# Feature-map attention and a soft mixture of experts: middle tiles summed in halves of 64 rows, with a bank of their own

## The chip, the cores and the metric

The kernel runs on one NeuronCore of a Trainium2 chip, in one launch. The metric is the device time of that launch in microseconds (us): the median of the runs. The profile is one further execution; its span goes from the first to the last instruction of the program. The engines are PE (TensorE; its weight loads are listed as PEld), DVE (VectorE), ACT (ScalarE), POOL (GpSimd) and SP (SyncE), which issues nearly all transfers.

## The reference

Linear attention over 8 batches, 8 heads, 576 tokens and 64 dimensions, then a soft mixture of 8 experts with 4 slots each over the 4608 resulting rows of 512. Everything is float32. The first part is where the change lies:

```python
def phi(x):
    proj = np.einsum('bhsd,df->bhsf', x, w_phi)          # w_phi: 64 x 128
    proj = proj - np.max(np.abs(proj), axis=-1, keepdims=True)
    return np.concatenate([np.exp(proj), np.exp(-proj)], axis=-1)
q_p, k_p = phi(q), phi(k)
kv = np.einsum('bhsf,bhsd->bhfd', k_p, v)                # per head: 256 x 64
z = np.sum(k_p, axis=2)
num = np.einsum('bhsf,bhfd->bhsd', q_p, kv)
den = np.einsum('bhsf,bhf->bhs', q_p, z)[..., None] + 1e-06
attn = num / den
# then, on x = attn as 4608 x 512:
logits = x @ phi                                         # 512 x 32
slot_input = softmax(logits, axis=0).T @ x
slot_out[e] = relu(slot_input[e] @ w1[e]) @ w2[e]        # 8 experts, 4 slots each
out = softmax(logits, axis=1) @ slot_out
```

## The kernel before, in words

Two batches of one head make a unit `u` (32 units). Its 2 x 576 = 1152 tokens are nine tiles of 128 tokens, so the fifth tile, number 4, holds the last 64 tokens of the first batch in rows 0 to 63 and the first 64 of the second batch in rows 64 to 127. It is called the middle tile. The projections work on blocks `b` of four tiles, 72 in all, without regard to units; `pieces` lists the stretches of a block that lie in one unit.

What happens to a block and a unit, with the lines of the profile:

- `proj` (L281): PE multiplies w_phi with the keys of block b on one half of the 64 + 64 rows, and the queries of block b - 2 on the other half. Results are psk (features by column) and psq (features by row).
- `kmax` (L286, DVE) and `kfac` (L289, L290, ACT): the largest absolute value per token, and its two exponentials. `kneg_exp`, `kpos_exp` (L312, L315, ACT): the features kf. `qabs` (L343, DVE), `qpos`, `qneg` (L348, L351, ACT): the same for queries.
- `vals` (L301, POOL): the values, with a column of ones at the end (65 columns), times both exponentials, one copy for each sign, into vs. The value tile vt comes from memory with ten blocks of 65 columns for the nine tiles: the middle tile is there twice, once with zeros in rows 64 to 127 and once with zeros in rows 0 to 63.
- `kvmm` (L328, PE): for each tile, sign and half of the 128 features one matmul of 64 stationary and 65 moving columns adds to kvp, which holds [sign, batch, 65] for the unit in one PSUM bank. For the middle tile the moving side is 130 columns wide, so that the two zeroed copies go into both batches at once.
- `kvcopy` (L337): one copy of kvp, 260 columns, to kvs, by DVE and ACT in the turn d, a, a, d.
- `num` (L381, PE): query features times kvs, in groups of three tiles. `scale`, `comb` (L392, L397, DVE), `denom` (POOL), `recip` (DVE, L412) and `divide` (POOL, L427) finish the rows of x.

After each half of the 8 heads' rows the logits of four tiles are formed (transposes to psx at L734, psl at L438) and the running softmax is kept. After the last unit follow the last logits (zturn to zsi; `zst` at L629 and L631 multiplies pieces of acc, 128 stationary columns, by 32 or 1 moving columns), then both expert layers (hp L850, yp L925) and the outputs (pso L945).

The order of the work is written out by hand: `ORDER` is a string of one letter per step (`LETTERS`), and the steps are issued in just this order on every engine. `Plan.add` gives each step its predecessors (`after`) and the buffers that it takes (`get`) and gives back (`put`); these only check the string. The costs in `add` are not used when the kernel is built. PSUM banks: two for psk, two for psq, one for kvp, and three (`nm`) which num, transposes, logits and slot sums share.

Of the kernel before, what the change touches and what calls it, by code (L numbers as in the profile page):

```python
# [56 lines left out]
class Plan:
# [42 lines left out]
ORDER = (  # L100
    "bcceafeefedhdggehjibecikbajelfcmdbmdknghjefomilcbunhfipoghclrjqddlrmkjagmjsnbkifnthijgvovmwcljofpwqdgcrvrmkjwnlm"
    "yhksomfdpnathixrvwvczolijwgfcrlhaqkdAvAgrmjnAbkwfbyomstizhcArfvwnlkjnAdorimdavAgcowhjpiqvcgwdfbmhgjyrlrdslxjztvf"
    "AknmivhiknawgowmcofjplcAhrjrAmdvqwxdlgjiykfrnakmgmostcvnbhpvjiwwlfocdjzqsArlvhkntrgbmdwAAvwomkfigcdryjharvznfkmi"
    "bowcvlpwjrghAqrmdnlijAAykofsmnhiczotxjvwgkdlvcfmgAwjqfjparrhsdmnmvgAtwAojlxihmkvyzwnorvjwpbrvwcfAixckmybdfazAnrh"
    "AdgliABABgjljCoqxcBCskhtBCmilmnfCdrDEkonvchpFwgvlwqoibcrrjdjkafbAnmhodsvkmwBitgCBcBvwCxlBylCfrnhfjrivmvhCwjDGdzx"
    "oEcwaqkipsndoFcgglHGjHIJrIymfKhKkAgldnqgbtLisojmArAvwfhkvimtpnjcojwzcrfalhvdgrmdwlkfAAnmAbjmJvwhoprkvMwyirjgjzcv"
    "wnlyAoifcdamdkqAnmlhixgzfoxsAtjrhjLviwrcgvlbmknoArfawvAjpqwxhycmklfbmnshrkdzidAtnorvcwAlivggjocmfajwrqMAprjdvhwk"
    "mknsdiynmgrAtzjfAogclvAwhoAljfiqdvgcwmrhkjpdvsftwxlnryvmgimazwrhkbjvowrnaiAvAmjpwocckymfnzdbAAhrdglBNjlCBgoiqCkf"
    "cBbsBAjmthAifmlnCrCdkhnvjiwxvwoDcoaEcBpbFbdgflBjxhrdCrNmvqxmskfnwCiBlCBhtgCojicaGxvfklDrnwdohxOrEkgnjFqvwiymvpcw"
    "gocHjHdzmIfgyrzJGkIsdlKLhnKmAfArjhlAmtvwiovAkiwAcnAjobacpqdgfglsrrvhmfjbknltwvOwmdyrvkjjgnraxvwimwzphocikocdfyrl"  # L110
    "ghirAdjqnlkszPxAAmfonojtmjvhwigmcvwdMjpcNArrflagkdmqhnsimfgljAkhAmvtwjopcfvyrJwjbirlanqdzkmAmAvvhnocsoAMiwtwbgcf"
    "yzbAjralNlfvhwAkrdiAmdkpnbxnvoghroqvjgwjcwdfsligycxtrdkzhvrminmvoAfjlmawgjcrfLApwlbjhvkqwryhmkAminzonAsBBcodticA"
    "gCCvdfjwBCfBrlrhlCAdkvniokhmjvnqxiwbDgwcoOEcFBBprlglsajytdmCmvjmxqknCfwPzHpgBIBjChmCrsjdgjfoPJvrkiDwhvEwKncFiMbd"
    "fGAohcHLylrtlgkaIqmAmJndsgKoijcfAzvwrdNkpvfwnrbvmAwahjhlirogAAtriknvjwvcwGyfOljzxkdonoxcmmghlqpriAvwbkrbjdysxAmA"
    "tznrcfhvgkndvwiwjofcaAlAlmmrhgpqdAkvfrjmwsnMohriitayLckvocvnwgrkdwnvjwxmjzffAglmplocyhjhAzNocxxAAqRldSRlmjrsmgkS"
    "APjOtPvmqprwvRrwSnvwiOTURsAQRkSotyrSnRvoVQwRVzrSSrvwyyTAARUzPASvzARXASwyXRYzA4XZYSY0X2QYZ0TZ73W905Q5682236573Q5+"
    "695W5888++8/W+<=/Q!=!i!!")

# [7 lines left out]
def tile_kernel(ctx: ExitStack, tc, xT, vv, w, phi, w1, w2, cst, out):  # L126
# [166 lines left out]
    def vals(p):  # L293
        b, u, t0, t1 = pieces[p]
        v = vt[u].rearrange("p (t e) -> p t e", e=65)
        if b not in vs:
            vs[b] = vp.tile([128, 2, 5, 65], F32, tag="vs", name="vs", bufs=BUFS["vs"])
        g = NT * u - 4 * b
        for t, n, o in (t0, min(t1, 5) - t0, 0), (max(t0, 4), t1 - max(t0, 4), 1):
            if n > 0:  # L300
                nc.gpsimd.tensor_tensor(vs[b][:, :, place(b, u, t, o):place(b, u, t, o) + n],  # L301
                                        v[:, t + o:t + o + n].unsqueeze(1).broadcast_to([128, 2, n, 65]),
                                        km[b][:, 0:2, g + t:g + t + n].unsqueeze(3).broadcast_to([128, 2, n, 65]), op=ALU.mult)

    def place(b, u, t, o):

        g = NT * u + t
        return g - 4 * b + (o if t == 4 else any(x % NT == 4 for x in range(4 * b, g)))

# [7 lines left out]
    def kvmm(p):  # L317
        b, u, t0, t1 = pieces[p]
        if t0 == 0:
            kvp[u] = pkv.tile([128, 2, 2, 65], F32, tag="kv", name="kvp")  # L320
        ps = kvp[u].rearrange("p a b e -> p a (b e)")
        v2 = vs[b].rearrange("p a t e -> p a (t e)")
        for t in range(t0, t1):
            o, m = 65 * (t > 4), 130 if t == 4 else 65
            at = 65 * place(b, u, t, 0)
            for pn in range(2):
                for f in range(0, FE, FE // 2):
                    nc.tensor.matmul(  # L328
                        ps[f:f + FE // 2, pn, o:o + m],
                        kf[b][:, pn, NT * u + t - 4 * b, f:f + FE // 2],  # L330
                        v2[:, pn, at:at + m],
                        start=(t == 0 and pn == 0), stop=(t == NT - 1 and pn == 1),
                        skip_group_check=True)

    def kvcopy(u, d):
        kvs[u] = qp.tile([128, 2, 2, 65], F32, tag="kvs", name="kvs")
        (nc.vector.tensor_copy if d else nc.scalar.copy)(kvs[u], kvp.pop(u))  # L337

# [675 lines left out]
```

## Time and profile before

| | |
|---|---|
| median of 3 runs | 329.23 us (328.81 to 330.84) |
| the profiled execution's own time | 328.39 us |
| its span | 326.6 us, mean granted TensorE clock 0.993 |
| busy: PE, PEld, DVE, ACT, POOL | 315.7, 269.4, 241.2, 229.3, 160.9 us |
| kvmm on PE (L328) | 2304 records, from 10.5 to 254.2 us |
| num on PE (L381) | 2304 records |
| projections on PE (L281) | 576 + 576 records |

A matmul of the program in float32 leaves two records in the profile, each with its weight load. A shape such as "128\*64 128x65" is rows by columns of the stationary operand, then rows by columns of the moving one. Two matmuls on different halves of the array (128\*64: different columns; 64\*128: different rows) can run side by side, so durations of records add up to more than the time; starts tell how fast they follow each other.

### The profile page before, as it was taken

To read this page: it belongs to the slowest core of one execution; us is meant where nothing else is said; L and a number is where in the kernel's file an instruction comes from. 1 tells how busy PE (TensorE), PEld (TensorE's weight loads), DVE (VectorE), ACT (ScalarE), POOL (GpSimd) and SP (SyncE) were. 2 spreads that over 40 slices of the span, in tenths; PEclk is the share of its full clock that TensorE was granted. 3 is DMA by queue.
4 is the path that set the end of the run, shared out by engine and by line. 5 is a ranking of instruction groups with operands and counts; after the bars stand their busy time and mean duration, and the time that the engine had idled before them with its cause. 6 is when DMAs were issued, how large, how long until landed. Compare 5 with 4: busy or idle time off the path is not lost.

```text
span 326.6 us, 16706 instructions
## 1 busy us (share of the span) xinstructions
PE 315.7 (97%) x7095; PEld 269.4 (82%) x7095; DVE 241.2 (74%) x688; ACT 229.3 (70%) x674; POOL 160.9 (49%) x339
## 2 busy tenths in 40 slices
PE   8999999999999999999999999999999999999990
...
GB/s 248 198 173 175 171 207 121 235 198 207 215 96 185 199 204 141 235 171 244 169 170 174 174 225 192 223 51 237 188 223 258 320 354 310 412 409 366 323 377 298
DMA packets 23130, 74.12 MB, mean 227 GB/s; under 512 B 2576, under 2 KB 2960, under 8 KB 23056
## 3 DMA queue, kind: packets, MB, share of 16 engines
...
q10 hardware_dynamic: 288, 0.40, 0.4%
q14 instruction: 18, 0.15, 0.1%
...
## 4 chain that ended last, share of the span: by engine, by line
PE 93%; DVE 1%; ACT 1%; issue 1%; DMA 1%; SPq 0%; DVEq 0%; POOL 0%; ACTq 0%; POOLq 0%
PE kvp L328 24%; PE psn L381 22%; PE psq L281 12%; PE psk L281 11%; PE psx L734 5%; PE yp L925 4%; PE hp L850 4%; PE psl L438 3%; PE pso L945 2%; PE pss L470 2%; PE psw L206 2%; DMA out<-o 1%; PE psd L463 1%; PE pss L585 1%; PE psh L903 1%
## 5 line engine op out<-in xcount | busy, mean ns | idle before, releaser
L301 POOL TENSOR_TENSOR vs<-vt,mk 128x520 f32<-128x520 f32 (+3 forms) x128 | 91.5, 730 | 59.5 <-ACT mk L290 42.5
L328 PE MATMUL kvp<-vs,kf 128*64 128x65 f32 (+1 forms) x2304 | 85.7, 229 | 0.0
L328 PEld LDWEIGHTS kvp<-vs,kf 128*64 128x64 f32 x2304 | 78.6, 138 | 4.7 <-issue 1.9
L381 PE MATMUL psn<-kvs,qf 128*64 128x65 f32 x2304 | 79.2, 223 | 0.3 <-issue 0.2
L381 PEld LDWEIGHTS psn<-kvs,qf 128*64 128x64 f32 x2304 | 72.6, 138 | 4.5 <-issue 1.0
L281 PE MATMUL psq<-xs,wd 64*128 64x128 f32 x576 | 75.5, 280 | 0.0
L281 PE MATMUL psk<-wd,xs 64*128 64x128 f32 x576 | 75.3, 280 | 0.1
L281 PEld LDWEIGHTS psq<-xs,wd 64*128 64x128 f32 x576 | 67.2, 187 | 4.1 <-issue 2.1
L281 PEld LDWEIGHTS psk<-wd,xs 64*128 64x128 f32 x576 | 67.0, 187 | 3.1 <-issue 1.6
L286 DVE TENSOR_REDUCE mk<-psk 128x4 f32<-128x512 f32 x72 | 48.2, 679 | 15.9 <-ACT kf L312 9.1
L312 ACT ACTIVATE kf<-psk 128x512 f32<-128x512 f32 x72 | 42.6, 594 | 22.5 <-PE psk L281 8.0
L343 DVE TRANSPOSE_TENSOR_REDUCE mts<-psq 128x16 f32<-128x512 f32 x72 | 50.2, 706 | 8.2 <-PE psq L281 3.5
L348 ACT ACTIVATE qf<-psq 128x512 f32<-128x512 f32 x72 | 42.4, 592 | 10.7 <-PE psn L381 3.0
L427 POOL TENSOR_TENSOR xc<-un,dn 128x256 f32<-128x256 f32 x62 | 37.9, 614 | 13.3 <-DVE dn L412 7.0
L351 ACT ACTIVATE qf<-psq 128x512 f32<-128x512 f32 x72 | 42.4, 594 | 1.7 <-DVE mts L343 1.7
L315 ACT ACTIVATE kf<-psk 128x512 f32<-128x512 f32 x72 | 42.6, 595 | 0.5 <-DVE mk L286 0.5
L392 DVE TENSOR_TENSOR un<-psn,eq 128x195 f32<-128x195 f32 x96 | 33.0, 350 | 10.3 <-PE psn L381 7.5
L397 DVE TENSOR_TENSOR un<-psn,un 128x195 f32<-128x195 f32 x96 | 33.4, 354 | 1.9
L359 ACT ACTIVATE mh<-mts 32x36 f32<-32x36 f32 x128 | 29.4, 229 | 2.4 <-DVE mts L343 0.6
L365 DVE TENSOR_REDUCE eq<-mh 32x9 f32<-32x36 f32 x128 | 26.1, 204 | 5.2 <-ACT mh L359 3.9
L949 DVE COPY o<-pso 128x384 f32<-128x384 f32 x24 | 12.1, 552 | 13.0 <-PE pso L945 13.0
L949 ACT COPY o<-pso 128x384 f32<-128x384 f32 x24 | 10.2, 484 | 11.7 <-PE pso L945 10.7
...
## 6 DMA issues: line engine op xcount, KB each, us to landing
...
```

The lines of the kernel that those rows point to most:

```text
L281: nc.tensor.matmul(ps, l, r, start=True, stop=True)
L286: nc.vector.tensor_reduce(km[b][:, 2], kx[b], axis=AX, op=ALU.max, apply_absolute_value=True)
L301: nc.gpsimd.tensor_tensor(vs[b][:, :, place(b, u, t, o):place(b, u, t, o) + n], v[:, t + o:t + o + n].unsqueeze(1).broadcast_to([128, 2, n ...
L312: nc.scalar.activation(kf[b][:, 1], kx[b], AF.Exp, scale=-1.0)
L315: nc.scalar.activation(kf[b][:, 0], kx[b], AF.Exp)
L328: nc.tensor.matmul(ps[f:f + FE // 2, pn, o:o + m], kf[b][:, pn, NT * u + t - 4 * b, f:f + FE // 2], v2[:, pn, at:at + m], start=(t == 0 an ...
L343: nc.vector.tensor_reduce(mts.rearrange("p r j -> p j r")[:, o:o + 4], qx[b].rearrange("p j (r t) -> p (j r) t", t=32), axis=AX, op=ALU.ma ...
L348: nc.scalar.activation(qf[b][:, 0], qx[b], AF.Exp)
L351: nc.scalar.activation(qf[b][:, 1], qx[b], AF.Exp, scale=-1.0)
L381: nc.tensor.matmul(ps[64 * f:64 * f + 64, j, pn], q2[:, pn, 64 * f:64 * f + 64], kv[:, pn, b2], start=True, stop=True)
L397: nc.vector.tensor_tensor(x, nx.pop(s)[:, :, 1], x, op=ALU.add)
L427: divider(u).tensor_tensor(x[:, :, h * D:(h + 1) * D], un[u][:, a:b, 0:64], dn[u][:, a:b].unsqueeze(2).broadcast_to([128, b - a, 64]), op= ...
```

## The change

- The values come with nine blocks of 65 columns, without the zeroed copies (`VW` 585 in place of 650), vs holds four tiles in place of five, and `vals` is one POOL instruction a piece.
- `kvmm` leaves out the middle tile. A new step `mid` does it in halves of 64 rows: for each sign, rows 0 to 63 add to the first batch in kvp with all 128 features as stationary columns, and rows 64 to 127 write the second batch's share into a bank of its own, psi (`half`), one of the three shared `nm` banks.
- `kvcopy` is cut in three: `mcopy` (ACT) copies psi to part2; `kvcopy` (always ACT now) copies the first batch's half of kvp; `kvadd` (DVE) adds part2 to the second batch's half. The first num group of a unit needs kvcopy, the others kvadd.
- `kf` and `vs` are given back by a step of no work, `kfree`, after kvmm and mid.
- `ORDER` is written anew throughout.

```diff
-VW = 10 * 65
+VW = NT * 65
+VSW = 2 * 4 * 65
@@ vals
-            vs[b] = vp.tile([128, 2, 5, 65], F32, tag="vs", name="vs", bufs=BUFS["vs"])
-        for t, n, o in (t0, min(t1, 5) - t0, 0), (max(t0, 4), t1 - max(t0, 4), 1):
-            if n > 0:
-                nc.gpsimd.tensor_tensor(vs[b][:, :, place(b, u, t, o):place(b, u, t, o) + n],
...
+            vs[b] = vp.tile([128, 2, 4, 65], F32, tag="vs", name="vs", bufs=BUFS["vs"])
+        g, n = NT * u - 4 * b, t1 - t0
+        nc.gpsimd.tensor_tensor(vs[b][:, :, g + t0:g + t1],
...
@@ kvmm
-            o, m = 65 * (t > 4), 130 if t == 4 else 65
-            for pn in range(2):
+            for pn in range(2) if t != 4 else ():
                 for f in range(0, FE, FE // 2):
                     nc.tensor.matmul(
-                        ps[f:f + FE // 2, pn, o:o + m],
-                        kf[b][:, pn, NT * u + t - 4 * b, f:f + FE // 2],
-                        v2[:, pn, at:at + m],
+                        kvp[u][f:f + FE // 2, pn, t > 4],
+                        kf[b][:, pn, at, f:f + FE // 2],
+                        vs[b][:, pn, at],
+    def mid(u):
+        b = (NT * u + 4) // 4
+        at = NT * u + 4 - 4 * b
+        half[u] = bank3(("mid", u), [128, 2, 65], "psi")
+        for pn in range(2):
+            nc.tensor.matmul(kvp[u][:, pn, 0], kf[b][0:64, pn, at], vs[b][0:64, pn, at], start=False, stop=True, skip_group_check=True)
+            nc.tensor.matmul(half[u][:, pn], kf[b][64:128, pn, at], vs[b][64:128, pn, at], start=True, stop=True)
+    def mcopy(u):
+        nc.scalar.copy(part2, half.pop(u))
-    def kvcopy(u, d):
+    def kvcopy(u):
         kvs[u] = qp.tile([128, 2, 2, 65], F32, tag="kvs", name="kvs")
-        (nc.vector.tensor_copy if d else nc.scalar.copy)(kvs[u], kvp.pop(u))
+        nc.scalar.copy(kvs[u][:, :, 0], kvp[u][:, :, 0])
+    def kvadd(u):
+        nc.vector.tensor_tensor(kvs[u][:, :, 1], kvp.pop(u)[:, :, 1], part2, op=ALU.add)
@@ ORDER (one line of each)
-    "bcceafeefedhdggehjibecikbajelfcmdbmdknghjefomilcbunhfipoghclrjqddlrmkjagmjsnbkifnthijgvovmwcljofpwqdgcrvrmkjwnlm"
+    "bcadfchediefbeeeghgcljfeiejcmh~adeikkmbgjjnnmodcflhio?pbb~dgckj@:rfmrlhg~qnodjkafmishml?ptviwcn@ovuxg~jjfwlr:rkd"
```

The new order shows on PE at a place in the early middle of the program. Before, a unit's kvmm with its middle stands between num and two projections in a row; psk and psq alternate in the left-out rows, eight pairs of rows in one stretch:

```order
L381 MATMUL psn<-kvs,qf 64x65 x24
L328 MATMUL kvp<-vs,kf 64x130 x4
L328 MATMUL kvp<-vs,kf 64x65 x16
L281 MATMUL psk<-wd,xs 128x128
L281 MATMUL psq<-xs,wd 128x128
...
L381 MATMUL psn<-kvs,qf 64x65 x24
L328 MATMUL kvp<-vs,kf 64x65 x12
```

In the changed kernel, at about the same place, a projection (four pairs of rows) stands alone or behind the middle (`mid`, L332 and L333), and kvmm and num are split around it:

```order
L320 MATMUL kvp<-vs,kf 64x65 x24
L389 MATMUL psn<-kvs,qf 64x65 x24
L332 MATMUL kvp<-vs,kf 128x65
L333 MATMUL psi<-vs,kf 128x65
...
L283 MATMUL psq<-xs,wd 128x128
L283 MATMUL psk<-wd,xs 128x128
...
L320 MATMUL kvp<-vs,kf 64x65 x8
L389 MATMUL psn<-kvs,qf 64x65 x24
```

What moved: the middle left the run of kvmm and joined that of the projection, and two projections that stood together now have kvmm and num between them.

On ACT, at the place of one unit's copy, before (mk are the factors of keys, kf their features, qf the queries'):

```order
L315 ACTIVATE kf<-psk 128x512
L337 COPY kvs<-kvp 128x260
L449 ACTIVATE eT,es<-psl,low_134 128x128
L451 ACTIVATE co<-low_133,low_134 128x1
L453 COPY lT<-psl 128x128
```

and after:

```order
L292 ACTIVATE mk<-mk 128x4
L338 COPY part_138<-psi 128x130
L752 COPY xT<-psx 128x512
L307 ACTIVATE kf<-psk 128x512
L342 COPY kvs<-kvp 128x2x65
L310 ACTIVATE kf<-psk 128x512
```

The one copy of 260 columns became two of 130 on ACT with other work between them. The third part is DVE's, at the same place of the program, after:

```order
L405 TENSOR_TENSOR un<-psn,un 128x195
L345 TENSOR_TENSOR kvs<-kvp,part_138 128x2x65
L288 TENSOR_REDUCE mk<-psk 128x4
L351 TENSOR_REDUCE mts<-psq 128x4x4
L373 TENSOR_REDUCE eq<-mh 32x9 x4
```

The sum stands in DVE's queue ahead of kmax (L288) and qabs (L351).

More of the change, by code (lines that the diff above doesn't have):

```diff
@@ L45 @@
 BUFS = {'xs': 3, 'kf': 3, 'vs': 2, 'vt': 2, 'qf': 3, 'un': 2, 'xT': 4, 'xc': 2}
-PICK = {'xcopy': 'adda', 'kvcopy': 'daad', 'zde': 'a'}
+PICK = {'xcopy': 'adda', 'zde': 'a'}
 TOP = 212900
 def room(bufs):
-    parts = [bufs["xs"] * XW * 4, bufs["kf"] * 4096 + bufs["vs"] * 2624 + bufs["vt"] * 2624,
-             bufs["qf"] * 4096 + 2 * 1056 + 512, bufs["un"] * 2368, bufs["xT"] * 2048, (bufs["xc"] + 1) * G * DM * 4]
+    parts = [bufs["xs"] * XW * 4, bufs["kf"] * 4096 + bufs["vs"] * VSW * 4 + bufs["vt"] * VW * 4,
+             bufs["qf"] * 4096 + 2 * 1056 + 512 + 544, bufs["un"] * 2368, bufs["xT"] * 2048, (bufs["xc"] + 1) * G * DM * 4]
     return [int(n) // 4096 for n in np.cumsum([TOP - sum(parts)] + parts)]
@@ L105 @@
[L105 to L114, printed above, removed]
@@ new lines @@
+    "rAmryAshkn~tvgiocjwkdnfhlzcajiov?jmmr~A@gfwlApb:cvjwdqmksmAxr~ynr?abolzgtfvhdijkcAwvmrwjhl@ginodpv:q~jArcfhsmgdt"
+    "Ak~mvwinfx?oglchak~jl@nwqojbmdbrvirpa:ykzcmwjvwArsrf?hyA~gAndlzofticmgkxj~v@avjnkhm~iopwdwrAglq:frjsvnchiwAyktmd"
+    "~oArnflcgvhwzjxiod?kbc@fmhAmvljwlrAAapg:~rvwkmnnq~jidfmyzA?Aoos@hcABCifltvBcCgj~dBhlgjqBmwCdpxCrvrgwjk:vfDwEisbh"
+    "nrFommtkn~BaCBciocv?wGC~HBIjjdkngCBmbxKl@ClfLDyjrpx:hErizmqvfFkndhJoogwHsicIvx?GtcA~AwKrfdagylAz@vLrkvnkhnmjwomr"
+    "d~lfAbhv~icpAwjqo:gdwiglcAm~srbjxtfhxkdryvknwmaljzfjmonivor?pvahAwc~lgwf@:AiqkcdyrlrjsnAdmgtvhmk~fhzjowjvAg?iAcn"
@@ new lines @@
+    "md~b@p:fbalrojbicvmmwwhgdkqn~jArmyikstlogfcvwxz?hjriMnldpA@Avrow~qcvk:rm~fnhgoadjimj?fckgswAlt~dv@hmbnxgfraypl:h"
+    "woiqzvjckn~dmAiwlsjA~grorvct?wArfyjhmdvknowvjf@zJmkbwplghAi:cAl~brqviAwrjnsMftymmd~okrnzogvhvcwiAwx?c@faANlk~dfl"
+    "BAdgCBrjhmCagjvbjpwBiq:BrCymCDnsh~o?kcnEtj@FxBBkm~lmCdCogiBvpnCxwGB:cfCfDlordrEjjqvhmFzvmiwHkwnh~NyHO?I@ci~gfzos"
+    "ItaldcljKKAGrfLgdqAAxkvnrwhjomvhiLAgpcw~xsrdAblvtk:rnfwAkbgvnjiocPmhrw~ajiyJmlzofmhcdkjvniw?gloAcxpJ@~jdA:qrkfnr"
+    "mohvM~ifwsmglyAtr?aNzcjdMjvwk~vAmwhli@nOrpfrAbgqk:nvwdoomg~xAsjchriljfkmnydzmthg?obpOavcAvw@~lwicfbrhdarj:Aqikbj"
@@ new lines @@
+    "xlgmvm?dsnk~fgoh~AjPcnw@motdypfvlw:rPzj~vAwiqckhnsirrvAAwdgtfmrvwgjoy~jrvwzAlxhvkAnAociammwd?yczpAf@hBlj:kCnBxdm"
+    "~iABlgCBocjqfCrlkCb~fAsdgnhrmkojtvm?hwiiv~cl@pDw:anrbqEavkdbgojjrFwcxBsfBnlmdmt~yoC?hviGgfc@xjBCahCBmCxgjpkDlnb:"
+    "~wzmfrEFirHvhkwnIqHKjIvAdgAwoiLJs~jKcltfhdo?cr@rkNAymvmnzwgvG~dal~fMokALpicghqnwrrjk:mdJjosvitlwAc~Abfvwh?xgrnfj"
+    "xmkvinadlowhyjmzcr@gpMA~lbfAoq:ivcmAkjdwnrsrog~dhty?iclkOf@vjwhnzvmo~mrwjpilgardAq:kvnfAwhmjsgi~rAcktov?bnwvdwgy"
+    "crmxjfkzlnvwmjx~lofpyocd@c:hlAqsmgzr~AjlAhrjmAkmnNtARvvQwwSR?pQk@SRRqO:nrSvTw~SPAyoRSsUrztAvRwySRSrvwyrNovQTzAwz"
@@ L166, in tile_kernel @@
               for u in range(4 * b // NT, (4 * b + 3) // NT + 1)]
-    qx, nx, qf, qe, mh, un, dn, xc = ({} for _ in range(8))
+    qx, nx, qf, qe, mh, un, dn, xc, half = ({} for _ in range(9))
     sent = []
@@ L296, in vals @@
         if b not in vs:
-            vs[b] = vp.tile([128, 2, 5, 65], F32, tag="vs", name="vs", bufs=BUFS["vs"])
-        g = NT * u - 4 * b
-        for t, n, o in (t0, min(t1, 5) - t0, 0), (max(t0, 4), t1 - max(t0, 4), 1):
-            if n > 0:
[L301 to L308, printed above, removed]
+            vs[b] = vp.tile([128, 2, 4, 65], F32, tag="vs", name="vs", bufs=BUFS["vs"])
+        g, n = NT * u - 4 * b, t1 - t0
+        nc.gpsimd.tensor_tensor(vs[b][:, :, g + t0:g + t1],
+                                v[:, t0:t1].unsqueeze(1).broadcast_to([128, 2, n, 65]),
+                                km[b][:, 0:2, g + t0:g + t1].unsqueeze(3).broadcast_to([128, 2, n, 65]), op=ALU.mult)
     def kneg_exp(b):
@@ L320, in kvmm @@
             kvp[u] = pkv.tile([128, 2, 2, 65], F32, tag="kv", name="kvp")
-        ps = kvp[u].rearrange("p a b e -> p a (b e)")
-        v2 = vs[b].rearrange("p a t e -> p a (t e)")
         for t in range(t0, t1):
-            o, m = 65 * (t > 4), 130 if t == 4 else 65
-            at = 65 * place(b, u, t, 0)
-            for pn in range(2):
+            at = NT * u + t - 4 * b
+            for pn in range(2) if t != 4 else ():
                 for f in range(0, FE, FE // 2):
                     nc.tensor.matmul(
-                        ps[f:f + FE // 2, pn, o:o + m],
-                        kf[b][:, pn, NT * u + t - 4 * b, f:f + FE // 2],
-                        v2[:, pn, at:at + m],
+                        kvp[u][f:f + FE // 2, pn, t > 4],
+                        kf[b][:, pn, at, f:f + FE // 2],
+                        vs[b][:, pn, at],
                         start=(t == 0 and pn == 0), stop=(t == NT - 1 and pn == 1),
                         skip_group_check=True)
-    def kvcopy(u, d):
+    def mid(u):
[5 more added lines that the diff above has]
+            nc.tensor.matmul(half[u][:, pn], kf[b][64:128, pn, at], vs[b][64:128, pn, at], start=True, stop=True)
+    part2 = qp.tile([128, 2, 65], F32, name="part2", bufs=1)
+    def mcopy(u):
+        nc.scalar.copy(part2, half.pop(u))
+    def kvcopy(u):
         kvs[u] = qp.tile([128, 2, 2, 65], F32, tag="kvs", name="kvs")
-        (nc.vector.tensor_copy if d else nc.scalar.copy)(kvs[u], kvp.pop(u))
+        nc.scalar.copy(kvs[u][:, :, 0], kvp[u][:, :, 0])
+    def kvadd(u):
+        nc.vector.tensor_tensor(kvs[u][:, :, 1], kvp.pop(u)[:, :, 1], part2, op=ALU.add)
     mts = const.tile([128, 4, 4 * NT], F32, name="mts")
@@ L641, in tile_kernel @@
     plan = Plan(dict({k: BUFS[k] for k in ("kf", "vs", "qf", "un", "xT", "xc", "vt")}, xs=BUFS["xs"] - 2, psk=2, psq=2,
-                     kb0=1, kb1=1, qb0=1, qb1=1, pkv=1, kvs=2, psn=2, mo=2, mk=6, mh=1, eq=3, dn=3, lT=3, de=2,
+                     kb0=1, kb1=1, qb0=1, qb1=1, pkv=1, kvs=2, psn=2, mo=2, mk=6, mh=1, half=1, eq=3, dn=3, lT=3, de=2,
                      cd=3, pl=2, pr=3, nm=3))
@@ L647, in tile_kernel @@
         first = e < 2
-        add("load", e, SP, 1.35 if e else 1.43, (lambda: None) if first else lambda e=e: xload(e), lat=2.2, at=8 / 3 * e,
+        add("load", e, SP, 1.35 if e else 1.6, (lambda: None) if first else lambda e=e: xload(e), lat=2.2, at=8 / 3 * e,
             get=[] if first else ["xs"], after=[("vload", 0)] if e == 1 else [])
@@ L667, in tile_kernel @@
                 n = t1 - t0
-                mid = t0 <= 4 < t1
-                task("vals", POOL, 0.14 * (1 + (mid and t1 > t0 + (t0 == 4))) + 0.22 * (n + mid), vals, p, b,
+                task("vals", POOL, 0.14 + 0.22 * n, vals, p, b,
                      after=[("kfac", b), ("vload", u)] + ([] if pieces[p - 1][0] != b else [("vals", p - 1)]),
                      get=["vs"] * (p == 0 or pieces[p - 1][0] != b), put=["mk"] * end + ["vt"] * (t1 == NT))
-                task("kvmm", PE, 0.233 * n + 0.215 * mid, kvmm, p, b, after=[("kpos_exp", b), ("vals", p)] + ([("kvmm", p - 1)] if p else []),
-                     get=["pkv"] * (t0 == 0), put=["kf", "vs"] * end, mode="c", lat=0.25)
+                task("kvmm", PE, 0.233 * (n - (t0 <= 4 < t1)), kvmm, p, b, after=[("kpos_exp", b), ("vals", p)] + ([("kvmm", p - 1)] if p else []) + ([("spin", NSPIN - 1)] if p == 3 else []),
+                     get=["pkv"] * (t0 == 0), mode="c", lat=0.25)
+                if t0 <= 4 < t1:
+                    first = next(i for i, x in enumerate(pieces) if x[1] == u)
+                    task("mid", PE, 0.23, mid, u, b, after=[("kpos_exp", b), ("vals", p), ("kvmm", first)], get=[("nm", ("mid", u))], mode="r", lat=0.25)
+                    task("mcopy", ACT, 0.17, mcopy, u, b, after=[("mid", u)], get=["half"], put=[("nm", ("mid", u))], lat=0.1)
+                if end:
+                    near = [v for v in range(NU) if (NT * v + 4) // 4 == b]
+                    task("kfree", None, 0.0, lambda b: None, b, b, after=[("kvmm", p)] + [("mid", v) for v in near], put=["kf", "vs"], lat=0.0)
         q, bank = b - 2, [f"qb{b % 2}"]
@@ L691, in tile_kernel @@
         if end:
-            d = pick("kvcopy") == "d"
             p = max(i for i in range(len(pieces)) if pieces[i][1] == u)
-            task("kvcopy", DVE if d else ACT, 0.34 if d else 0.27, lambda u, d=d: kvcopy(u, d), u, after=[("kvmm", p)], get=["kvs"], put=["pkv"])
+            task("kvcopy", ACT, 0.17, kvcopy, u, after=[("kvmm", p), ("mid", u)], get=["kvs"], lat=0.1)
+            task("kvadd", DVE, 0.21, kvadd, u, after=[("kvcopy", u), ("mcopy", u)], put=["pkv", "half"], lat=0.1)
             task("qfac", ACT, 0.86, qfac, u, after=[("qabs", b) for b in range(NT * u // 4, (NT * u + NT - 1) // 4 + 1)], get=["mh"])
```

17 lines of the change are left out of this document (5 added, 12 removed), and 2 rows, old and new, of the table LETTERS.

## The prediction

> **What bounds the kernel now.** I read the page's busy shares, its slices and its chain first, then a table by stretches, and last TensorE's (PE's) instructions one by one. In the page, part 1, the digits of part 2 and the chain of part 4:
>
> ```profile
> PE 315.7 (97%) x7095; PEld 269.4 (82%) x7095; DVE 241.2 (74%) x688; ACT 229.3 (70%) x674; POOL 160.9 (49%) x339
> PE   8999999999999999999999999999999999999990
> PE 93%; DVE 1%; ACT 1%; issue 1%; DMA 1%; SPq 0%; DVEq 0%; POOL 0%; ACTq 0%; POOLq 0%
> ```
>
> A busy share of 97% alone proves little, since matmuls overlap. The chain does: 93% of it lies on PE. By stretches (columns: length, then busy time of PE, PEld, DVE, ACT, POOL, then the granted clock, the share of the DMA engines and GB/s):
>
> ```profile
> 12.00:70.00 58.00, 58.00 (x1501) 55.27 (x1499) 46.63 (x128) 49.78 (x147) 38.70 (x79) 1.00 0.63 187
> 100.00:130.00 30.00, 30.00 (x814) 28.99 (x814) 26.00 (x71) 25.11 (x76) 22.24 (x48) 1.00 0.62 188
> 200.00:235.00 35.00, 35.00 (x790) 30.92 (x788) 29.23 (x83) 27.40 (x84) 18.73 (x40) 1.00 0.55 166
> ```
>
> From 12 to 235 us PE is never idle and has its full clock. The other engines have slack: DVE is busy 26.00 of 30.00 us and ACT 25.11 in the densest stretch. So here the time is the sum of what PE issues, and every edit counts by its PE time, unless it makes PE wait. To price PE work I take starts, not durations. The timeline of PE (start, time until the last one ends, count):
>
> ```profile
> 27.94 1.62 PE L381 MATMUL psn<-kvs,qf 128*64 128x65 f32 x48
> 29.39 1.55 PE L328 MATMUL kvp<-vs,kf 128*64 128x65 f32 x40
> 30.87 0.37 PE L281 MATMUL psk<-wd,xs 64*128 64x128 f32 x1
> ...
> 31.09 0.27 PE L281 MATMUL psk<-wd,xs 64*128 64x128 f32 x1
> ...
> 31.75 0.27 PE L281 MATMUL psk<-wd,xs 64*128 64x128 f32 x1
> ...
> 31.96 1.62 PE L381 MATMUL psn<-kvs,qf 128*64 128x65 f32 x48
> ```
>
> and, from the chain in order of time, two runs with no switch inside:
>
> ```profile
> 17.02 2.31 PE kvp L328 x72
> ...
> 37.58 1.40 PE psn L381 x48
> ```
>
> A matmul of the program is two records. The two column halves of a tile run side by side, so one tile of num (8 records, four pairs) takes 1.40/6 = 0.233 us, 0.058 us a pair. A whole unit of kvmm is nine tiles in 2.31 us: eight at 0.233, so **the middle tile with its 130 columns takes 0.446 us**. Projections start every (31.75 - 31.09)/6 = 0.11 us, again two side by side (psk and psq on opposite row halves).
>
> **What a change of array shape costs.** The stretch of halves by columns (128*64) from 27.94 to 30.87 is 2.93 us; its content is six num tiles (1.40), four kvmm tiles (0.93) and a middle (0.446), 2.78 together. The excess is 0.15 us. The projection (64*128) from 30.87 to 31.96 is 1.09 us for eight pairs at 0.11, excess 0.20 us. So each run of the first shape costs 0.15 us above its content, and each of the second 0.20.
>
> **The middle tile after the change.** It becomes 4 matmuls, 8 records: for each sign one on rows 0-63 into kvp and one on rows 64-127 into psi, each with a stationary operand of 128 columns and 65 moving columns. If they pair like the projections, there are four steps. Their length is the disputed number, as no row of before has 64 rows, 128 stationary and 65 moving columns. If the moving columns set it, it is the 0.058 us of a num pair, and the middle takes 0.233 us. If the weight load sets it, I need a row with 128 stationary columns and few moving ones. There is one, zst (L629, 32 moving columns; L631 has 1). Their weight loads, and the mean load of three shapes by line and form:
>
> ```profile
> 271.84 0.52 PEld L629 LDWEIGHTS pst<-sf,acc 128*128 128x128 f32 x4 [0.66 <-DVE acc L591]
> ...
> 272.86 0.30 PEld L631 LDWEIGHTS pst<-ssum,sf 128*128 128x128 f32 x2
> ```
>
> ```profile
> L328 PEld LDWEIGHTS kvp<-vs,kf 128*64 128x64 f32 x2304 | 78.6, 138 | 4.7 <-issue 1.9 <-POOL xc L427 0.8
> L281 PEld LDWEIGHTS psk<-wd,xs 64*128 64x128 f32 x576 | 67.0, 187 | 3.1 <-issue 1.6 <-ACT kf L315 0.6 <-ACT mk L290 0.2
> L629 PEld LDWEIGHTS pst<-sf,acc 128*128 128x128 f32 x8 | 1.1, 190 | 0.7 <-DVE acc L591 0.7
> ```
>
> Four loads in 0.52 us, the last of 0.19: one every 0.11 us with 32 moving columns, and (0.30 - 0.19) = 0.11 with one. The moving columns do not matter there; 128 stationary columns in f32 take 0.11 us. Halving the rows does not help: 64 rows by 128 columns load in 187 ns, 128 rows by 128 in 190, and 128 by 64 in 138. So I take 0.11 a step, and the middle costs 4 x 0.11 = **0.44 us, what it cost before**. The bounds are 0.233 and 0.45 us; over 32 units the edit is worth from -6.8 to +0.1 us, and I take 0.
>
> The Trainium skill, "TensorE: Matmul & The Clock Gate", section "LDWEIGHTS (loading the stationary operand)", says the load goes by the stationary columns and not by the contraction rows, P / 1.2 ns: by it a step is an estimated 107 ns and the middle 0.43 us, a gain of 0.5 us in all. The rows give 0.11 and no gain.
>
> **The new order on PE.** Counted over the two instruction lists, PE changes its shape 29 times more: runs of halves by columns go from 49 to 63, runs of halves by rows (projections and middles) from 44 to 59, and the other shapes keep 71. Before, 28 of the 44 row runs held two projections back to back; now 14 of 59 do. Of the 32 middles only one stands alone between other shapes, so it is not the middle itself but the split projections that add runs. Cost: 14 x 0.15 + 15 x 0.20 = **5.1 us**, all on the path, since PE has nothing idle to hide it.
>
> **The copies.** The nearest rows, by line and form:
>
> ```profile
> L337 DVE COPY kvs<-kvp 128x260 f32<-128x260 f32 x16 | 6.7, 419 | 2.0 <-PE kvp L328 1.9
> L337 ACT COPY kvs<-kvp 128x260 f32<-128x260 f32 x16 | 6.0, 377 | 1.5 <-PE kvp L328 1.5
> L453 ACT COPY lT<-psl 128x128 f32<-128x128 f32 x6 | 1.6, 260 | 0.0
> L392 DVE TENSOR_TENSOR un<-psn,eq 128x195 f32<-128x195 f32 x96 | 33.0, 350 | 10.3 <-PE psn L381 7.5 <-POOL eq L368 0.9 <-POOL xc L427 0.8
> ```
>
> ACT gets mcopy and kvcopy in every unit, each near the 260 ns of L453: 32 x 0.52 - 6.0 = +10.6 us. DVE gets a sum of 130 columns, below the 350 ns for 195 and above nothing known; at 0.30 us it is 32 x 0.30 - 6.7 = +2.9 us. ACT goes from 25.11 to about 26.4 of 30 us in the densest stretch. It stays covered by PE; if that cover were gone, the rival on waits below has the price. The added waits: kvadd stands in DVE's queue until ACT has done both copies, and behind it stand kmax and qabs, which free the projection's banks. num of the second and third group waits for kvadd, the first for kvcopy, and the next unit's kvmm for both. By the order's rows, at least one num tile group of 0.70 us (24 records) or a projection stands between, against 0.26 to 0.6 us of copying. I take 0; below nothing is not excluded, as the old copy of 0.42 us was longer than the 0.30 us sum. mid also takes one of three PSUM banks that num and the transposes share, until mcopy, some 0.7 us (0.44 and a copy of 0.26) in every unit. I take 0, and a lost num overlap for a few units as the upper end.
>
> **POOL and DMA.** vals drops the doubled middle: 96 instructions in place of 128, nine blocks in place of ten. Its four shapes:
>
> ```profile
> L301 POOL TENSOR_TENSOR vs<-vt,mk 128x520 f32<-128x520 f32 x32 | 33.8, 1055 | 23.3 <-ACT mk L290 19.1 <-issue 4.0
> L301 POOL TENSOR_TENSOR vs<-vt,mk 128x130 f32<-128x130 f32 x32 | 12.9, 404 | 5.4 <-ACT mk L290 2.8 <-PE kvp L328 1.6 <-POOL vs L301 0.6
> ```
>
> The slope is (1055 - 404)/3 = 217 ns a block over a base of 187, so 288 x 0.217 + 96 x 0.187 = 80 us instead of 93. POOL waits 19.1 us on ACT ahead of the widest shape alone, so the 13 us only become more waiting. Each of the 32 value loads shrinks by a tenth, and they lie in stretches with the DMA engines at 0.55 to 0.63 by the rows above. Both count 0. The weight loads keep their slots, and the tail from 256 us on keeps its instructions.
>
> **The sum.** The profiled execution took 328.39 us, of which the span is 326.6. Middle 0, shapes +5.1, copies, POOL and DMA 0: 333.5. The median of the runs is 0.84 higher than the profiled one, and runs lie between 328.81 and 330.84; I put the forecast at **333.7 us**. For queues that fit better or worse than before I allow -2 and +3: 331.7 to 336.7.
>
> **Rivals.** *The middle goes at the speed of its moving columns.* Then 328.4 + 5.1 - 32 x (0.446 - 0.233) = 326.7 us, which is not slower. For it: the work in the array is half. Against it: the two steps of 0.11 in L629 and L631, and the 187 ns load. It decides if the step in the new records is under 0.10. Chance 0.10. The Trainium skill, "TensorEngine Tiling (Array Packing)", section "Theoretical Speedup", gives up to twice the speed for a small dimension of at most 64, which is this case; the row that bears on it, L629, speaks for a load-bound step, so I leave it at that chance.
>
> *The single kvp bank makes PE wait.* If mcopy or kvcopy comes late in ACT's queue (behind exponentials of 0.59 us), kvadd holds DVE and then num holds PE. At one exponential in every third to half of the units, 11 to 16 x 0.59, it adds 6 to 9 us, less some 2 that the groups of 0.70 us in between absorb, so 4 to 7 on the 333.5: 337.5 to 340.5. For it: two handovers more, ACT 10.6 us busier. Against it: DVE and ACT still have over 10% free. Chance 0.10.
>
> *The new order removes waits.* PE's uninterrupted busy time can hide short waits between starts; the 5.1 us may be paid partly from those. The page's 1% of the chain under "issue" (3.3 us) is the most: 330.2 to 331.7. Chance 0.10.
>
> The forecast itself has 0.70. A measurement of this kernel tells about 1% from no change: faster is under 325.9, slower over 332.5. Of the forecast's 0.70 a seventh lies below 332.5. Slower: 0.60 + 0.10 = 0.70, less a little for all four being estimates, 0.68. Within 1%: 0.10 + 0.10 and most of the first rival, 0.28. Faster: 0.04. The range takes the forecast's band and most of the third rival, and leaves out the first and most of the second: 330.0 to 337.0.
>
> **What would show it.** In the profile after, kvp and psi records of 64*128 with 65 columns should start every 0.11 us per pair, and their loads take about 187 ns; 0.06 us refutes the main step. Row runs should cost 0.20 and column runs 0.15 above content, with 15 and 14 more of them. PE should again be busy in all of 12 to 235 us, and the last kvp record should start some 5 us later than the 254.2 of before:
>
> ```profile
> L328 PE MATMUL kvp<-vs,kf x2304: 217/222/325, 10.5 to 254.2; 128*64 128x65 f32 x160, 128*64 128x130 f32 x32
> ```
>
> I am wrong if the loads of the two row halves overlap in another way than the projections', or if PE shows idle time ahead of num.

## The result, and the profile after

The changed kernel takes 334.54 us (median of 4 runs, 334.27 to 334.74) against 329.31 us of the kernel before in the same series: a ratio of 1.015, 95% interval 1.0116 to 1.0184, so 5.2 us more; the forecast was 333.7. The profiled execution took 334.6 us with a span of 332.8, 6.2 us longer than the span of before; the profiled execution of before was 0.9 us faster than its median, which is why the traces differ by more than the medians. All medians and ratios here and below leave out the three runs in the chip's slower state (one of halves_slack, two of quarters_fewer_runs).

From its page, the busy shares, the slices of PE and the chain's shares:

```profile
PE 320.7 (96%) x7095; PEld 271.9 (82%) x7095; DVE 243.0 (73%) x704; ACT 236.6 (71%) x722; POOL 149.9 (45%) x307
PE   8999999999999999999999999999999999999990
PE 91%; DVE 4%; ACT 1%; issue 1%; DVEq 0%; POOL 0%; ACTq 0%; POOLq 0%
```

The same stretches as before (length, busy PE, PEld, DVE, ACT, POOL, clock, DMA share, GB/s):

```profile
12.00:70.00 58.00, 57.98 (x1456) 55.03 (x1457) 46.68 (x130) 51.48 (x160) 34.89 (x69) 1.00 0.57 177
100.00:130.00 30.00, 30.00 (x754) 28.42 (x752) 24.62 (x70) 27.02 (x87) 18.60 (x38) 1.00 0.60 186
200.00:235.00 35.00, 34.73 (x765) 30.33 (x762) 26.40 (x75) 27.68 (x88) 15.58 (x30) 1.00 0.53 169
```

PE is again the bound: 30.00 of 30.00 us, with 754 matmul records where there were 814. It is as full as before and does less in the same time. What a middle costs now can be read from its timeline, here for a middle right behind a projection and ahead of a change of shape:

```profile
30.86 0.37 PE L283 MATMUL psk<-wd,xs 64*128 64x128 f32 x1
...
31.75 0.27 PE L283 MATMUL psk<-wd,xs 64*128 64x128 f32 x1
...
31.86 0.22 PE L332 MATMUL kvp<-vs,kf 64*128 64x65 f32 x1
...
31.92 0.27 PE L332 MATMUL kvp<-vs,kf 64*128 64x65 f32 x1
...
32.03 0.27 PE L332 MATMUL kvp<-vs,kf 64*128 64x65 f32 x1
...
32.14 0.27 PE L332 MATMUL kvp<-vs,kf 64*128 64x65 f32 x1
...
32.35 1.85 PE L320 MATMUL kvp<-vs,kf 128*64 128x65 f32 x56
```

The middle starts every 0.11 us, like the projections ahead of it, although it moves 65 columns where they move 128. Only its second pair comes sooner, 0.06 us behind the first; the loads of all 32 middles start 0.108 to 0.113 us apart, without such an exception. In this trace a row run of one projection lasts 1.092 us. With a middle ahead of the projection it lasts 1.539: the middle is 0.447 us, and it was 0.444 before. With the middle last, as here from 30.86 to 32.35, it lasts 1.486, so such a middle costs 0.394 us; this holds for 8 of the 32. The loads by line and form:

```profile
L333 PEld LDWEIGHTS psi<-vs,kf 64*128 64x128 f32 x128 | 16.6, 188 | 0.0
L332 PEld LDWEIGHTS kvp<-vs,kf 64*128 64x128 f32 x128 | 16.6, 187 | 1.6 <-issue 0.5
```

187 and 188 ns, as the projections' 187.

To see where the 6.2 us lie I added up, in both traces, the time from the first start of each run of one array shape to the first start of the next, and took off the content priced as in the prediction (what is left above content and shape price is called waits):

| PE shape | before: runs, us | after: runs, us |
|---|---|---|
| halves by columns (kvmm, num) | 49, 150.1 | 63, 137.6 |
| halves by rows (projections, middles) | 44, 74.4 | 59, 91.4 |
| full (transposes, f32) | 32, 26.7 | 31, 28.2 |
| 32 columns | 27, 48.3 | 27, 48.1 |
| waits within the first two | 3.1 | 2.8 |

Columns lose 12.5 us (the middles, 32 x 0.444 = 14.2, less 14 runs more at 0.15), rows gain 17.0 (the middles, 24 x 0.447 + 8 x 0.394 = 13.9, and 15 runs more at 0.20). Together +4.5. Another 1.5 us is in the full shape. The largest single part of it, 0.64 us, is one run of transposes right after the last middle (start, length, line; the bracket is idle time ahead and what ended it); 0.67 more is in two runs at 86.5 and 222.8 us:

```profile
260.08 0.66 PE L748 MATMUL psx<-cs,xc 128*128 128x128 f32 x4
261.16 0.66 PE L748 MATMUL psx<-cs,xn 128*128 128x128 f32 x4 [0.42 <-ACT part L338]
```

The transpose at 261.16 needs the bank that psi holds until mcopy (L338) has read it.

### The profile page after: what moved, and what is told of

It is laid out like the page before. It is cut to its first block, busy times and chain, and to the rows that moved or that the text cites. A ratio compares the mean times of both kernels' runs of the same rounds, so it can differ in the third digit from the quotient of the medians.

```text
span 332.8 us, 16738 instructions
## 1 busy us (share of the span) xinstructions
PE 320.7 (96%) x7095; PEld 271.9 (82%) x7095; DVE 243.0 (73%) x704; ACT 236.6 (71%) x722; POOL 149.9 (45%) x307
## 4 chain that ended last, share of the span: by engine, by line
PE 91%; DVE 4%; ACT 1%; issue 1%; DVEq 0%; POOL 0%; ACTq 0%; POOLq 0%
PE psn L389 20%; PE kvp L320 19%; PE psk L283 11%; PE psq L283 11%; PE yp L939 5%; PE psx L748 5%; PE kvp L332 4%; PE hp L864 4%; PE pso L959 3%; PE psl L446 2%; PE pss L478 2%; PE psw L208 2%; PE pss L593 1%; PE psd L471 1%; DVE un L405 1%
## 5 line engine op out<-in xcount | busy, mean ns | idle before, releaser
L301 POOL TENSOR_TENSOR vs<-vt,mk 128x520 f32<-128x520 f32 (+3 forms) x96 | 79.8, 837 | 53.7 <-ACT mk L292 35.5
L283 PE MATMUL psk<-wd,xs 64*128 64x128 f32 x576 | 79.8, 282 | 0.2 <-ACT kf L310 0.2
L283 PE MATMUL psq<-xs,wd 64*128 64x128 f32 x576 | 80.0, 282 | 0.0
L320 PE MATMUL kvp<-vs,kf 128*64 128x65 f32 x2048 | 72.5, 224 | 0.3 <-DVE kvs L345 0.2
L283 PEld LDWEIGHTS psk<-wd,xs 64*128 64x128 f32 x576 | 68.7, 188 | 3.1 <-issue 1.2
L283 PEld LDWEIGHTS psq<-xs,wd 64*128 64x128 f32 x576 | 68.9, 188 | 2.8 <-issue 1.8
L320 PEld LDWEIGHTS kvp<-vs,kf 128*64 128x64 f32 x2048 | 65.2, 138 | 4.7 <-issue 1.8
L351 DVE TRANSPOSE_TENSOR_REDUCE mts<-psq 128x16 f32<-128x512 f32 x72 | 51.0, 709 | 13.2 <-PE psq L283 4.1
L288 DVE TENSOR_REDUCE mk<-psk 128x4 f32<-128x512 f32 x72 | 48.8, 680 | 14.9 <-PE psk L283 11.0
L435 POOL TENSOR_TENSOR xc<-un,dn 128x256 f32<-128x256 f32 x62 | 38.1, 614 | 18.8 <-DVE dn L420 12.5
L332 PE MATMUL kvp<-vs,kf 64*128 64x65 f32 x128 | 19.6, 273 | 0.0
```

The lines of the kernel that those rows point to most:

```text
L283: nc.tensor.matmul(ps, l, r, start=True, stop=True)
L288: nc.vector.tensor_reduce(km[b][:, 2], kx[b], axis=AX, op=ALU.max, apply_absolute_value=True)
L301: nc.gpsimd.tensor_tensor(vs[b][:, :, g + t0:g + t1], v[:, t0:t1].unsqueeze(1).broadcast_to([128, 2, n, 65]), km[b][:, 0:2, g + t0:g + t1] ...
L320: nc.tensor.matmul(kvp[u][f:f + FE // 2, pn, t > 4], kf[b][:, pn, at, f:f + FE // 2], vs[b][:, pn, at], start=(t == 0 and pn == 0), stop=( ...
L351: nc.vector.tensor_reduce(mts.rearrange("p r j -> p j r")[:, o:o + 4], qx[b].rearrange("p j (r t) -> p (j r) t", t=32), axis=AX, op=ALU.ma ...
L435: divider(u).tensor_tensor(x[:, :, h * D:(h + 1) * D], un[u][:, a:b, 0:64], dn[u][:, a:b].unsqueeze(2).broadcast_to([128, b - a, 64]), op= ...
```

## The experiments

The theory: PE's issue time sets the end; a middle in halves costs what the doubled one cost, as its step is a load of 128 stationary columns; the loss is the shape changes of the new order. The rivals: the moving columns set the step; or the halves, their copies and the bank are the loss and the order is harmless. The ratios are to the kernel before on the same chip.

**Fewer moving columns.**

```diff
-            nc.tensor.matmul(kvp[u][:, pn, 0], kf[b][0:64, pn, at], vs[b][0:64, pn, at], ...)
+            nc.tensor.matmul(kvp[u][:, pn, 0, 0:33], kf[b][0:64, pn, at], vs[b][0:64, pn, at, 0:33], ...)
```

and the same for psi and its copy; part2 is set to zero once at the start. The other 32 value columns of the middle tiles are left out of the result.

> The changed kernel with the moving side of the middle cut from 65 to 33 columns in both halves; the other 32 value columns of the middle tiles are left out of the sums. If the weight load of 128 stationary columns sets the step, a middle stays at 4 x 0.11 = 0.45 us and the time at 334.5 us. If the moving columns set it, a step falls from 0.11 to about half, 32 x 4 x 0.05 = 7 us less: 327.5 us.

Measured: 333.75 us, ratio 1.0139 (1.0075 to 1.0203), where the rival expected 327.5. PE's timeline at a middle that stands last ahead of a change of shape:

```profile
30.33 0.37 PE L283 MATMUL psk<-wd,xs 64*128 64x128 f32 x1
...
31.32 0.19 PE L332 MATMUL kvp<-vs,kf 64*128 64x33 f32 x1
...
31.36 0.27 PE L332 MATMUL kvp<-vs,kf 64*128 64x33 f32 x1
...
31.47 0.27 PE L332 MATMUL kvp<-vs,kf 64*128 64x33 f32 x1
...
31.58 0.27 PE L332 MATMUL kvp<-vs,kf 64*128 64x33 f32 x1
...
31.79 1.85 PE L320 MATMUL kvp<-vs,kf 128*64 128x65 f32 x56
```

With half the moving columns the step is still 0.11 us: the loads start 0.108 to 0.112 us apart, and a run with the middle ahead of a projection still lasts 1.538. Only the middles that stand last ahead of a change of shape get shorter, by 0.027 us (the run lasts 1.459 in place of 1.486). The moving columns do not set the step.

**Fewer stationary columns.**

```diff
         for pn in range(2):
+            for f in range(0, FE, FE // 2):
+                o = slice(f, f + FE // 2)
-            nc.tensor.matmul(kvp[u][:, pn, 0], kf[b][0:64, pn, at], ...)
+                nc.tensor.matmul(kvp[u][o, pn, 0], kf[b][0:64, pn, at, o], ...)
...
```

> The changed kernel with each half of the middle cut once more by its stationary columns: eight matmuls of 64 rows, 64 stationary and 65 moving columns a unit in place of four with 128 stationary columns, the whole sum still computed. If the load sets the step, four quarters run side by side in steps of 0.058 us, and a middle takes 0.23 us in place of 0.45, 6.8 us less in all. If 64 by 64 is one more shape, it adds some 38 runs of 0.15 to 0.20 us, 5.7 to 7.6 us, and the total stays at 333.5 to 335.5 us; if the array counts it as the shape of the projections, nothing is added and it comes to 327.7 us. If the load did not matter, it would be slower, 340 us.

Measured: 335.18 us, ratio 1.0159 (1.0127 to 1.0192). The loads by form, and one middle in PE's timeline:

```profile
L334 PEld LDWEIGHTS kvp<-vs,kf 64*64 64x64 f32 x256 | 10.2, 133 | 3.3 <-issue 0.5
```

```profile
39.97 0.27 PE L334 MATMUL kvp<-vs,kf 64*64 64x65 f32 x1
...
40.08 0.22 PE L334 MATMUL kvp<-vs,kf 64*64 64x65 f32 x1
...
40.14 0.22 PE L334 MATMUL kvp<-vs,kf 64*64 64x65 f32 x1
...
40.20 0.22 PE L334 MATMUL kvp<-vs,kf 64*64 64x65 f32 x1
...
40.36 1.15 PE L320 MATMUL kvp<-vs,kf 128*64 128x65 f32 x32
```

With 64 stationary columns the load takes 133 ns and the step falls to 0.06 us, four matmuls side by side. But 64 by 64 is a shape of its own: the run from 39.97 to 40.36 is 0.39 us (0.392 or 0.393 on nearly every one of the 32), so 0.233 of content and 0.16 of shape. And it splits the runs around it: row runs rise from 59 to 65. The gain of 6.8 us is eaten by the changes (32 x 0.16 and 6 x 0.20, together 6.3), which was the first of the two cases named. Moving and stationary columns together show that the load sets the step.

**The new order with the old middle.** The functions of before, with the letters and the order of the changed kernel; the steps mid, mcopy, kvadd and kfree do nothing, and ACT makes every copy of kvp.

```diff
-    "bcceafeefedhdggehjibecikbajelfcmdbmdknghjefomilcbunhfipoghclrjqddlrmkjagmjsnbkifnthijgvovmwcljofpwqdgcrvrmkjwnlm"
+    "bcadfchediefbeeeghgcljfeiejcmh~adeikkmbgjjnnmodcflhio?pbb~dgckj@:rfmrlhg~qnodjkafmishml?ptviwcn@ovuxg~jjfwlr:rkd"
...
+                    task("mid", None, 0.0, lambda u: None, u, b, lat=0.0)
```

> The kernel of before, with its doubled middle of 130 columns, but issued in the order of the changed kernel (the steps mid, mcopy and kvadd are empty, the copy is one by ScalarE). TensorE has 27 runs more than before, 14 by columns, 14 by rows, one of full shape less. If the order's shape changes are the cost, 14 x 0.15 + 14 x 0.20 = 4.9 us above before, less 0.15: 334.0 us. If the halves of the middle are the cost and the order is harmless: 329.3 us.

Measured: 334.24 us, ratio 1.0126 (1.010 to 1.0152), as the theory had it. The doubled middles are all there, and the last kvp record starts about where it does in the changed kernel. Here, then the changed kernel's kvmm and its middles:

```profile
L329 PE MATMUL kvp<-vs,kf x2304: 217/222/325, 11.1 to 259.1; 128*64 128x65 f32 x160, 128*64 128x130 f32 x32
```

```profile
L320 PE MATMUL kvp<-vs,kf x2048: 220/222/273, 10.7 to 258.3; 128*64 128x65 f32 x187
...
L332 PE MATMUL kvp<-vs,kf x128: 218/272/322, 14.2 to 259.9; 64*128 64x65 f32 x128
```

259.1, 258.3 and 259.9 us, against 254.2 before. So the order alone makes nearly all of the loss.

**The wait for the bank.**

```diff
-...R?pQk@SRRqO:...
+...R?@pQkSRRqO:...
```

> The changed kernel with one letter moved: the last unit's mcopy goes ahead of its kvcopy and of an exponential on ScalarE. In the trace a transpose waits 0.42 us for that copy near 261 us, since psi holds one of the three shared banks. If that wait is on the path, 0.4 to 0.9 us less: 333.6 to 334.1 us. If the next wait takes its place, no change: 334.5 us.

Measured: 334.26 us, ratio 1.0128 (1.009 to 1.0166). In the trace the wait is gone:

```profile
260.50 0.65 PE L748 MATMUL psx<-cs,xc 128*128 128x128 f32 x4
...
260.70 0.27 ACT L338 COPY part<-psi 128x130 f32<-128x130 f32 x1 [0.53 <-PE psi L333]
...
261.02 0.66 PE L748 MATMUL psx<-cs,xn 128*128 128x128 f32 x4
```

The second group follows the first by 0.52 us and no longer by 1.08, and the full shape falls from 28.2 to 27.6 us. In the time this is below what the intervals can tell; the end-to-end effect stays open.

**The halves in an order with fewer changes.** If the order is the loss, the halves must lose nothing in another order. Only `ORDER` differs from the changed kernel; its first line:

```diff
-    "bcadfchediefbeeeghgcljfeiejcmh~adeikkmbgjjnnmodcflhio?pbb~dgckj@:rfmrlhg~qnodjkafmishml?ptviwcn@ovuxg~jjfwlr:rkd"
+    "bccdfgaebeeeahieeeejdcfdhgknicjfgllmbohim~jfm?bcknajd~hiogcp@fbul:rqkdjldmg~jhnmfsrmihk?itnovwcvbojplwc~@fqgrdr:"
```

> The changed kernel, halves of 64 rows in a bank of their own and all, with the steps placed once more so that TensorE changes its shape less: 45 runs by columns (before 49, changed kernel 63), 45 by rows (44, 59), 29 of full shape (34, 34). If the splits of the order were the whole loss and the halves cost what the doubled middle cost, it is -4 x 0.15 + 0.20 - 5 x 0.15 = 1.2 us under before: 328.2 us, 6.3 us under the changed kernel. If the halves or the three copies cost something by themselves, it stays above before: 331 us or more.

Measured: 333.32 us, ratio 1.0112 (1.0082 to 1.0143). A miss: the runs are as counted, but the waits in column and row runs rose from 2.8 to 7.1 us. Two more were placed as densely, again by `ORDER` alone (first line shown).

The first is the quarters kernel in such an order:

```diff
-    "bcadfchediefbeeeghgcljfeiejcmh~adeikkmbgjjnnmodcflhio?pbb~dgckj@:rfmrlhg~qnodjkafmishml?ptviwcn@ovuxg~jjfwlr:rkd"
+    "bccedaefeegehjifeehdgebicfdklckmgdahnjnib~fjlmmjho?ocga@pl~fqi:dschrimrk~gjfmkjbdtnhml?pvnowg~aojc@bilfqcvrj:mwk"
```

> The same with the middle in quarters of 64 rows by 64 columns: 44 runs by columns, 42 by rows, 31 of full shape, and 32 of 64 by 64 with nothing else in them. A quarter run took 0.392 us in the other order, 0.05 less than the doubled middle: 32 x 0.05 = 1.7 us; shapes -5 x 0.15 - 2 x 0.20 - 3 x 0.15 = -1.6 us. Together 3.3 us under before: 326.2 us, faster than both kernels. If the copies or the bank make TensorE wait once it is this dense, it stays at 328 us or more.

Measured: 336.13 us, ratio 1.0193 (1.0148 to 1.0238). A miss: the sum of the changes said 326.2; PE waited.

The second is the kernel before in such an order:

```diff
-    "bcceafeefedhdggehjibecikbajelfcmdbmdknghjefomilcbunhfipoghclrjqddlrmkjagmjsnbkifnthijgvovmwcljofpwqdgcrvrmkjwnlm"
+    "bccedeagbedfbegeheieefchifcdkjaklhmgdnjonflbomijmhapicjcdkgljfrnbmqghdrlkjfsmngimuhtpjvowbclfoivqcwrkvjmrwndmslf"
```

> The kernel of before, doubled middle and all, placed once more in the same manner: 42 runs by columns (49), 41 by rows (44), 30 of full shape (34). If shape changes carry their price both ways, -7 x 0.15 - 3 x 0.20 - 4 x 0.15 = 2.3 us less: 327.2 us. If TensorE's order was not the limit, 329.5 us.

Measured: 334.91 us, ratio 1.0167 (1.0133 to 1.0201). A miss too: even the unchanged functions lose 5 us with fourteen runs fewer, where 2.3 us less was expected. In quarters_fewer_runs, then before, the times that the weight loads of kvmm waited (in total, times, longest):

```profile
PEld kvp L320 <- issue: 4.8, 9, 1.6
...
PEld kvp L320 <- POOL vs L301: 2.6, 6, 1.1
```

```profile
PEld kvp L328 <- issue: 1.9, 7, 0.8
```

In part, then, the kvmm loads wait for POOL's products (vs): 2.6 us in quarters_fewer_runs and 1.8 in before_fewer_runs. The rest stands under "issue", where the profile names no cause, and halves_fewer_runs has no such wait for vs. A reading that fits is that the longer a stretch of one shape is, the more of its operands must be ready at once; the runs do not show it for each wait.

**With slack.** The same three forms, placed to leave more time between a result and the PE step that reads it (`ORDER` alone, first lines shown). The changed kernel:

```diff
-    "bcadfchediefbeeeghgcljfeiejcmh~adeikkmbgjjnnmodcflhio?pbb~dgckj@:rfmrlhg~qnodjkafmishml?ptviwcn@ovuxg~jjfwlr:rkd"
+    "abccefefdehgdigbjeeheiccm~kjdfaglmhjlminbk?odc~bfenhgpljeaiocbrd@qfj:gm~bmkhrndjm?ifslok~ntv@vwocwhpfjgrl:rqakvd"
```

> The changed kernel placed once more, now leaving more time between a result on one engine and the TensorE step that reads it: 48 runs by columns (before 49, changed kernel 63), 50 by rows (44, 59), 30 of full shape (34, 34), 25 of 32 columns (27, 27). By runs it is -0.15 + 6 x 0.20 - 4 x 0.15 - 2 x 0.12 = +0.2 us to before, if it waits no more than before does: 329.8 us, against 334.5 us of the changed kernel. If the halves cost something by themselves, or the handover of the one kvp bank does, TensorE waits again as in the denser placing: 332 us or more.

The quarters kernel:

```diff
-    "bcadfchediefbeeeghgcljfeiejcmh~adeikkmbgjjnnmodcflhio?pbb~dgckj@:rfmrlhg~qnodjkafmishml?ptviwcn@ovuxg~jjfwlr:rkd"
+    "bcacdffeeeehedhgibeejebgcicfkdkmgh~jja?mldbln@~iofmpchnkdrj:gfiocghlmd~lqjrsfnkihnajtmmj?vvwocp@oi~fgcwl:drmjqrg"
```

> Quarters of 64 by 64, placed in the same manner: 53 runs by columns, 48 by rows, 33 of full shape, 28 of 32 columns, 32 of 64 by 64. Quarters -1.7 us, shapes +0.6 + 0.8 - 0.15 + 0.1 = +1.4 us: 0.3 us under before, 329.3 us, and up to 3 us less where the waits of before (some 3 us of TensorE's starts) go: 326.5 to 329.3 us. If waits come back as in the denser placing, 333 us or more.

The kernel before:

```diff
-    "bcceafeefedhdggehjibecikbajelfcmdbmdknghjefomilcbunhfipoghclrjqddlrmkjagmjsnbkifnthijgvovmwcljofpwqdgcrvrmkjwnlm"
+    "bccefhfeadedeegieebheicgcbdkjfglahmjlnmodkjjmpagjfinhcrlfqoikudgrcksmhjdntlbomjvmfnbwivhgjpaicwlobcfqrrkdmkmdgjv"
```

> The kernel of before placed in the same manner: 51 runs by columns, 45 by rows, 32 of full shape, 28 of 32 columns: 0.3 us more by runs, up to 3 us less by waits: 326.8 to 330 us. If it is as good as quarters_slack, the middle's form decides nothing and the order all; if it is 1.5 us or more behind, the quarters are worth their 1.7 us.

Measured, all kernels together, with the waits in runs of halves and quarters from the traces, in the manner of the table in the section on the result:

| kernel | column, row, 64 by 64 runs | waits, us | median, us | ratio |
|---|---|---|---|---|
| before | 49, 44, 0 | 3.1 | | 1 |
| changed | 63, 59, 0 | 2.8 | 334.54 | 1.015 (1.0116 to 1.0184) |
| old_middle_new_order | 63, 58, 0 | 3.2 | 334.24 | 1.0126 (1.010 to 1.0152) |
| quarters | 63, 65, 32 | 2.5 | 335.18 | 1.0159 (1.0127 to 1.0192) |
| halves_fewer_runs | 45, 45, 0 | 7.1 | 333.32 | 1.0112 (1.0082 to 1.0143) |
| quarters_fewer_runs | 44, 42, 32 | 13.3 | 336.13 | 1.0193 (1.0148 to 1.0238) |
| before_fewer_runs | 42, 41, 0 | 9.7 | 334.91 | 1.0167 (1.0133 to 1.0201) |
| halves_slack | 48, 50, 0 | 3.4 | 329.91 | 1.0027 (1.0003 to 1.005) |
| quarters_slack | 53, 48, 32 | 7.0 | 332.4 | 1.0087 (1.0061 to 1.0113) |
| before_slack | 51, 45, 0 | 5.5 | 330.89 | 1.0046 (1.0024 to 1.0067) |

halves_slack is the answer to the rival: the same halves, copies and bank as in the changed kernel, 4 us faster, 0.9 us (0.1 to 1.7) over before, where 0.2 over was expected by runs. It also has 24 runs fewer than the changed kernel at waits of 3.4 against 2.8 us, so the many splits of the changed kernel were not needed to keep PE fed. Its middles are unchanged:

```profile
L332 PE MATMUL kvp<-vs,kf 64*128 64x65 f32 x128 | 19.6, 273 | 0.0
```

The quarters never kept their 1.7 us: with 32 more runs their waits rose to 7.0 us. The other two were misses: 326.5 to 329.3 us was expected of quarters_slack and 326.8 to 330 of before_slack, by waits that would go, and the waits of both rose instead. No order that was tried beats the kernel before.

## Why the prediction was right

- **PE is the bound.** Right: 57.98, 30.00 and 34.73 us busy in the three stretches, and every experiment moved with PE's runs and waits.
- **The middle costs 0.44 us either way.** Right: 0.447 against 0.444, and 0.394 for the eight that stand last in their run, together 0.3 us less, which the prediction did not have. moving33 and quarters show the reason, the load of 128 columns. The rival of the moving columns falls. The Trainium skill, "TensorEngine Tiling (Array Packing)", section "Theoretical Speedup", has up to twice the speed for a dimension of at most 64; here 64 rows gave none, since the doubled form of before had used the array's column halves already and a step of halves by rows cost twice a step of halves by columns (0.11 against 0.058 us).
- **Shape changes, 5.1 us.** Right: old_middle_new_order shows 1.26% (1.0 to 1.5%), 4.2 us (3.3 to 5.0), where the same count gave 4.75 (4.9 - 0.15). The prices hold in the trace after: 16 records by rows last 1.09 us, 24 by columns 0.85.
- **Copies.** kvcopy 267 ns, mcopy 270 and kvadd 281, forecast 260, 260 and 300; ACT is busy 27.02 of 30 us in the densest stretch, forecast 26.4. They brought almost no wait to kvmm and num: 0.2 us of kvmm's idle time ends with kvadd, and the waits in halves fell from 3.1 to 2.8 us.
- **The bank.** Counted as 0, with a loss as the upper end; it was too low. The full shape took 1.5 us more; early_mcopy, which takes away the wait for psi's bank, has 0.6 of it less, and the rest the prediction had not foreseen. The waits that went and the eight shorter middles (0.3 us each) made up for part of it. So the sum, 333.5, came out 1.1 below the profiled execution's 334.6; that terms left out went both ways is luck.
- **POOL.** Right: 79.8 us for vals, forecast 80, and nothing gained from it.

The third rival, waits that go, had a small part (0.3 us); the second, the kvp handover, almost none in this order (0.2 us).
